# Filler matmuls of another size and number in the front of a fused linear-attention and gated-FFN kernel

## The chip, the core and the metric

The kernel runs on one core of a Trainium2 chip. The core has five engines with instruction streams of their own: TensorE (PE in the profile, with its weight loads as PEld), VectorE (DVE), ScalarE (ACT), GpSimd (POOL) and SyncE (SP). They meet through semaphores only. Sixteen DMA engines move data between the memory of the device and the core's on-chip memory; in this kernel SP and POOL issue the transfers. TensorE writes its results to PSUM, here eight banks of 128 partitions x 512 fp32 columns.

The metric is the time of one execution on the device in microseconds. A profiled execution also has a span, from the first to the last recorded instruction, which is a little shorter.

## The reference

Two parts, one after the other. The first is a gated linear attention over batch 4, 8 heads, 768 tokens and head dimension 48; the second is a feed-forward layer in which one projection is gated by the ReLU of another.

```python
f = 1.0 / (1.0 + np.exp(-f_logit))
for t in range(S):
    state = f[:, :, t, :, None] * state + np.einsum('bhd,bhe->bhde', k[:, :, t], v[:, :, t])
    y[:, :, t] = np.einsum('bhd,bhde->bhe', q[:, :, t], state)
...
x = y.transpose(0, 2, 1, 3).reshape(B * S, H * D)        # 3072 x 384
out = (np.maximum(x @ w_gate, 0.0) * (x @ w_val)) @ w_out  # 384 -> 1536 -> 384
```

## The kernel before

The sequence is cut into six chunks of 128 tokens. For each chunk and each pair of batches the attention is done in its chunked form. The logarithm of the gates is made on ScalarE (`bneg`) and summed over tokens by matmuls with triangular matrices (L594 for the first two chunks). Exponentials of the sums on ScalarE (L608) and products with k and q on VectorE and GpSimd (L610) give `hats`. TensorE transposes them (L642), VectorE copies them back (`qkT`, L650), and scores (L667), a mask (L683 on VectorE, L680 on GpSimd), the states (L692) and the output rows (L712, L717) follow. ScalarE writes these rows, transposed, as `xT` (L729). The feed-forward part of a chunk, for all four batches, reads `xT`: two projections on TensorE (L922), ReLU on ScalarE (L928), the product on VectorE (L932), the output projection on TensorE (L965, L945).

All matmul operands are bf16. Inputs are loaded by SP's queue (L487), in an order that is written out by hand; the weights come in three parts each through GpSimd's queue (L508), between GpSimd's computing steps: wg, wv, then wo. Some loads are written to wait for the landing of an earlier one.

The order of every engine's instructions is made by a small planner (class `Plan`): each operation has an estimated duration, a priority and tiles that it reads and writes; the planner simulates the engines and the DMA queues and gives each operation a start. From this it derives the order on each engine and the semaphore waits. An engine executes its list in this order, and a waiting instruction holds what stands behind it.

TensorE also gets *filler* matmuls. They multiply a tile of zeros with itself into the last PSUM bank, which the planner leaves alone until 15 us, and nobody reads their result. One of them (L1015) is an operation of the plan, at its start. The others are put in after planning: the loop over TensorE's order (L1027) looks at the planned gap ahead of each operation up to 15 us, and fills a share of it with matmuls of 512 columns. They are issued in front of that operation's semaphore wait (L1048), so TensorE works on them first and only then waits. In the order that results there are eighteen: two ahead of the matmul with `pick` (L434), seven ahead of the first sums (L594), six ahead of the first transposes (L642), one ahead of the scores (L667) and two ahead of the output rows (L712). The tile of zeros is cleared by VectorE's first instruction (`fill`, L415).

## Time and profile before

| | us |
|---|---|
| median of five runs | 192.71 |
| the five runs | 191.69, 192.32, 192.71, 194.14, 194.25 |
| the profiled execution, its time | 191.69 |
| its span | 190.0 |
| TensorE busy, share of the span | 182.5, 96% |
| first L594 matmul starts | 6.06 |
| first wv part waited for until | 17.63 |
| last wo part waited for until | 44.51 |

The page of the profile gives busy time per engine, groups of instructions by line, and the chain of waits that ended last. More detailed answers come from the trace: the chain in order of time, the timeline of one engine, and the work in a chosen stretch with the clock that TensorE was granted. In timeline rows the first number is the start in us from the beginning of the span, the second the time covered, then engine, line, operation, the tile written and the tiles read, the shape and the number of instructions. In brackets stands the idle time before and what ended it; "issue" there means that the profile shows nothing that was waited for.

### The profile page before, as it was taken

Reading aid. Unit: us, or ns where it says so; the run is one execution under the profiler, and the core shown is the slowest. Engines: PE = TensorE matmul, PEld = TensorE weight load, DVE = VectorE, ACT = ScalarE, POOL = GpSimd, SP = SyncE. Lnnn points to the kernel's source line nnn. Section 1 sums busy time; section 2 is a strip of 40 time slices with the busy share of each in tenths; the row PEclk is TensorE's granted clock in tenths of the full one; section 3 lists DMA queues with packets and bytes.
Section 4 is the critical chain, followed back from the end, with each engine's and each line's share of the span. In section 5 each row is a group of like instructions: output and inputs, shape, how many; then the busy total and the mean of one; then the engine's idle time right before and its main releaser. Section 6 shows DMA issues by size and latency. Waiting matters only on the chain.

```text
span 190.0 us, 5030 instructions
## 1 busy us (share of the span) xinstructions
PE 182.5 (96%) x2079; PEld 108.0 (57%) x2079; DVE 105.2 (55%) x189; ACT 109.6 (58%) x244; POOL 76.2 (40%) x109
## 2 busy tenths in 40 slices
PE   7887799999999999999999999999999999999994
PEld 2456684566685466768645564554555555554564
DVE  7799365995555856518695375625538233343300
ACT  3774459736598496575967739476533533334322
POOL 8496504771476638445393653615400000000000
PEclk9999999999999999999999999999999999999999
DMA  5999999999999999999999998999850310011113
GB/s 158 324 267 206 169 288 278 205 232 205 234 246 155 215 145 221 261 193 251 152 215 172 205 197 164 223 204 215 140 127 17 86 41 33 9 45 41 41 53 113
DMA packets 108854, 32.04 MB, mean 169 GB/s; under 512 B 101792, under 2 KB 108832, under 8 KB 108832
## 3 DMA queue, kind: packets, MB, share of 16 engines
q1 hardware_dynamic: 104848, 28.19, 73.5%
q0 software_dynamic: 3984, 3.54, 12.0%
q8 instruction: 16, 0.26, 0.5%
q14 instruction: 6, 0.05, 0.1%
HBM read 25.95 MB, written 4.72 MB: 161 GB/s over the span
## 4 chain that ended last, share of the span: by engine, by line
PE 82%; DMA 11%; POOL 3%; issue 1%; SPq 1%; ACT 0%; POOLq 0%
PE ps L922 48%; PE ps L965 23%; DMA wo<-in_moe_w_out_dram 5%; DMA wv<-in_moe_w_val_dram 4%; PE ps L852 3%; DMA q_in<-in_q_dram 2%; PE ps L817 2%; POOL hats L610 2%; PE ps L751 1%; PE ps L900 1%; POOL vpad L657 1%; PE ps L945 1%; PE ps L712 1%; SPq L487 1%; PE ps L754 0%
## 5 line engine op out<-in xcount | busy, mean ns | idle before, releaser
L932 DVE TENSOR_TENSOR gT<-relu,ps 128x512 bf16<-128x512 bf16 (+1 forms) x88 | 51.1, 588 | 61.0 <-PE ps L922 35.0
L928 ACT ACTIVATE relu<-ps 128x512 bf16<-128x512 f32 (+1 forms) x88 | 45.6, 522 | 28.2 <-PE ps L922 27.9
L922 PE MATMUL ps<-xT,wv 128*128 128x512 bf16 (+1 forms) x264 | 61.1, 340 | 0.4 <-DMA wv<-in_moe_w_val_dram 0.4
L922 PE MATMUL ps<-xT,wg 128*128 128x512 bf16 (+1 forms) x264 | 61.2, 340 | 0.0
L965 PE MATMUL ps<-wo,gT 128*128 128x384 bf16 x276 | 49.0, 326 | 0.2 <-DMA wo<-in_moe_w_out_dram 0.2
L965 PEld LDWEIGHTS ps<-wo,gT 128*128 128x128 bf16 x276 | 26.2, 98 | 18.2 <-DMA wo<-in_moe_w_out_dram 0.3
L922 PEld LDWEIGHTS ps<-xT,wv 128*128 128x128 bf16 x264 | 25.0, 98 | 19.6 <-DMA wv<-in_moe_w_val_dram 0.6
L922 PEld LDWEIGHTS ps<-xT,wg 128*128 128x128 bf16 x264 | 24.8, 98 | 19.5 <-issue 1.3
L975 ACT ACTIVATE osb<-ps 128x384 f32<-128x384 f32 x23 | 11.2, 495 | 26.2 <-PE ps L965 26.1
L827 DVE TENSOR_TENSOR ptm<-ps,tri 128x512 bf16<-128x512 f32 x32 | 20.5, 684 | 5.3 <-PE ps L817 5.2
L570 POOL TENSOR_TENSOR st<-ssum,dec 128x384 bf16<-128x384 f32 x16 | 13.1, 832 | 24.5 <-DVE ssum L568 24.4
L773 POOL TENSOR_TENSOR hats<-k_in,expo 128x384 bf16<-128x384 f32 x16 | 15.9, 1000 | 17.2 <-ACT expo L761 14.8
L777 POOL TENSOR_TENSOR hats<-q_in,expo 128x384 bf16<-128x384 f32 x16 | 15.7, 999 | 3.4 <-DMA q_in<-in_q_dram 3.3
L568 DVE TENSOR_TENSOR ssum<-ps,st 128x384 f32<-128x384 f32 x16 | 8.4, 553 | 3.7 <-PE ps L900 3.5
L683 DVE TENSOR_TENSOR ptm<-ps,mask 128x512 bf16<-128x512 f32 x14 | 8.7, 681 | 1.5 <-PE ps L667 1.4
L761 ACT ACTIVATE expo<-ps 128x384 f32<-128x384 f32 x16 | 7.9, 491 | 2.8 <-PE ps L754 2.7
L807 POOL CAST vpad<-v_in 128x384 bf16<-128x384 f32 x16 | 7.7, 507 | 1.8 <-DMA v_in<-in_v_dram 1.8
L763 ACT ACTIVATE expo<-ps 128x384 f32<-128x384 f32 x16 | 8.0, 500 | 0.0
L729 ACT ACTIVATE xT<-ps 128x384 bf16<-128x384 f32 x8 | 4.2, 599 | 5.4 <-PE ps L717 5.4
L742 ACT ACTIVATE f_in<-f_in 128x768 f32<-128x768 f32 x8 | 6.8, 844 | 0.9 <-DMA f_in<-in_f_logit_dram 0.9
L744 ACT ACTIVATE bneg<-f_in 128x768 bf16<-128x768 f32 x8 | 6.8, 846 | 0.1
L881 ACT ACTIVATE xT<-ps 128x384 bf16<-128x384 f32 x12 | 5.2, 486 | 2.5 <-PE ps L852 2.5
(85 smaller groups left out, 162.5 us busy)
## 6 DMA issues: line engine op xcount, KB each, us to landing
f_in<-in_f_logit_dram SPq DMA_DIRECT2D x12, 384.0 KB, 5.6
k_in<-in_k_dram SPq DMA_DIRECT2D x12, 384.0 KB, 5.4
q_in<-in_q_dram SPq DMA_DIRECT2D x12, 384.0 KB, 5.1
v_in<-in_v_dram SPq DMA_DIRECT2D x12, 384.0 KB, 5.4
out_dram<-osb SPq DMA_DIRECT2D x23, 192.0 KB, 2.4
wg<-in_moe_w_gate_dram POOLq DMA_DIRECT2D x3, 384.0 KB, 5.7
wv<-in_moe_w_val_dram POOLq DMA_DIRECT2D x3, 384.0 KB, 6.6
wo<-in_moe_w_out_dram POOLq DMA_DIRECT2D x3, 384.0 KB, 8.6
```

The lines of the kernel that those rows point to most:

```text
L568: add("DVE", lambda: ve.tensor_tensor(tmp[:, :], kv.ap[:, 0:HD], s_old[:, :], ALU.add), [kv, f"S{b}_{(c + 1) % 2}"], [key], prio=P + 8, ** ...
L570: add("POOL", lambda: gp.tensor_tensor(t4(s_new), t4(tmp), rate, ALU.mult), [key] + dk, [f"S{b}_{c % 2}"], prio=P + 8, **pool_t(HD))
L683: add("DVE", lambda i=i, j=j, mask=mask: ve.tensor_tensor(ptm[ms[i]][:, j, :, :], s[i][j].ap[:, :].rearrange("p (n t) -> p n t", n=NP), ma ...
L763: add("ACT", lambda: sc.activation(ex[:, 0, :], bc.ap[:, 0:HD], AF.Exp, scale=-1.0), [bc], [f"expq{ei // 2 * 2}_{ei % 2}"], prio=P + 1, ** ...
L773: add("POOL", lambda: gp.tensor_tensor(hk, kin[:, b % 2, :, :], ex[:, 1, :].rearrange("p (h d) -> p h d", h=H), ALU.mult), in_keys("k", c, ...
L777: add(e, lambda: engine[e].tensor_tensor(hq, qin[:, b % 2, :, :], ex[:, 0, :].rearrange("p (h d) -> p h d", h=H), ALU.mult), in_keys("q", ...
L827: add("DVE", lambda mi=mi, j=j, s=s: ve.tensor_tensor(ptm[mi][:, j, :, :], s.ap[:, :].rearrange("p (n t) -> p n t", n=NP), mask, ALU.mult) ...
L922: mm = te.matmul(bank.ap[:, 0:n], wt[:, kt, j * 128:(j + 1) * 128], xT[xi][:, kt, n0:n1], start=(kt == 0), stop=(kt == NK - 1))
L928: add("ACT", lambda: sc.activation(relu[ri][:, 0:n], gate.ap[:, 0:n], AF.Relu), [gate], [f"relu{ri}"], prio=P, **act_t(n))
L932: add("DVE", lambda: ve.tensor_tensor(gT[gi][:, j, n0:n1], relu[ri][:, 0:n], val.ap[:, 0:n], ALU.mult), [val, f"relu{ri}"], [f"gT{gi}_{j}_ ...
L965: mm = te.matmul(o[b].ap[:, 0:DM], gT[gi][:, j, b * C:(b + 1) * C], wo[:, j, :], start=(j == 0), stop=(j == NJ - 1))
L975: add("ACT", lambda b=b, oi=oi: sc.activation(osb[oi][:, :], o[b].ap[:, 0:DM], AF.Copy), [o[b]], [f"osb{oi}"], prio=P, **act_t(DM))
```

## The change

The fillers are no longer computed from the planned gaps by a formula. A list gives five groups, and each of the first five planned gaps over 0.4 us in TensorE's order takes one: nine fillers of 128 columns, eight of 512, five of 256, one of 512 and two of 512. With the filler that is part of the plan (now 128 columns wide) there are 26. They stand at the same five places as before. Columns beyond 128 are made by reading the same 128 columns of zeros again (a broadcast), so the tile of zeros has 128 columns instead of 512, and VectorE clears 64 words instead of 256 in each partition. The order of all real work is the same on all engines, but for two small clears of `dec` on VectorE that come before the products `upto` and `below` (L436) instead of after them.

```diff
-    zeros = sb("zeros", [128, 512], BF16)
+    zeros = sb("zeros", [128, 128], BF16)
...
-    fill("DVE", "zeros", zeros[:], 0.0, 256, -30)
+    fill("DVE", "zeros", zeros[:], 0.0, 64, -30)
...
-    WARM = 512
-    warm_until = 15.0
-    add("PE", lambda: te.matmul(banks[-1][:, 0:WARM], zeros[:, 0:128], zeros[:, 0:WARM]), ["zeros"], ["warm"], occ=0.2,
-        prio=-30)
+    add("PE", lambda: te.matmul(banks[-1][:, 0:128], zeros[:, :], zeros[:, :]), ["zeros"], ["warm"], occ=0.1, prio=-30)
...
-    def warm():
-        return te.matmul(spare[:, 0:WARM], zeros[:, 0:128], zeros[:, 0:WARM], start=True, stop=True, skip_group_check=True)
-
-    busy, at, begun = [], pl.free0["PE"], False
+    def warm(n):
+        return te.matmul(spare[:, 0:n * 128], zeros[:, :], zeros[:, :].unsqueeze(1).to_broadcast([128, n, 128]), start=True, stop=True,
+                         skip_group_check=True)
+
+    busy, at, wide = [], None, [(1, 9), (4, 8), (2, 5), (4, 1), (4, 2)]
     for op in order["PE"]:
-        gap, each = op.start - at, 0.44 if at < 4.0 else 0.23
-        if begun and op.start <= warm_until:
-            for _ in range(int((0.9 if gap > 1.5 else 0.6) * gap / each)):
-                busy.append((op, warm))
-        begun = True
+        gap = op.start - at if at is not None else 0.0
+        if wide and gap > 0.4:
+            n, many = wide.pop(0)
+            busy += [(op, lambda n=n: warm(n))] * many
         at = op.start + op.occ
```

## The prediction

> **What bounds the kernel now.** The profiled execution took 191.69 us: a span of 190.0 and 1.69 around it. The median of the five runs is 192.71, and they reach from 191.69 to 194.25, so the profile shows the best of them. I read the chain of waits first, in order of time, to learn where the front (the part before TensorE runs without a pause) touches the end.

> ```profile
> 7.54 1.00 POOL hats L610
> 8.55 0.90 POOL vpad L657 x2
> 9.45 0.88 POOL wg L508
> 10.32 7.30 DMA wv<-in_moe_w_val_dram
> ...
> 20.81 0.28 PE ps L717 x11
> 21.09 1.02 issue
> 22.11 0.22 PE ps L717
> ...
> 35.94 8.57 DMA wo<-in_moe_w_out_dram
> ```

> From 44.5 us on everything is TensorE, line after line, so the end is the moment at which that stretch starts plus about 143 us. Before it the chain runs through GpSimd (hats, vpad, then its weight transfers), through TensorE from 17.7 to 31.9 us, and through the last wo transfer. The fillers are not on it. They can move the end in two ways only: by the clock that they give the real matmuls, and by what stands behind them in TensorE's order. So I read the front's TensorE timeline next.

> ```profile
> 2.44 3.17 PE L1024 MATMUL ps<-zeros 128*128 128x512 bf16 x7
> ...
> 6.06 0.34 PE L594 MATMUL ps<-bneg,upto 128*128 128x384 bf16 x1 [0.46 <-ACT bneg L586]
> 6.23 0.33 PE L594 MATMUL ps<-bneg,below 128*128 128x384 bf16 x1
> 6.39 0.49 PE L594 MATMUL ps<-bneg,upto 128*128 128x384 bf16 x2
> 6.72 0.34 PE L619 MATMUL ps<-pick,bneg 128*128 128x2 bf16 x8
> 6.92 1.46 PE L1024 MATMUL ps<-zeros 128*128 128x512 bf16 x6
> 8.62 1.08 PE L642 MATMUL ps<-ident,hats 128*128 128x128 bf16 x16 [0.24 <-DVE hats L610]
> ```

> The seven fillers start (3.17 - 0.63)/6 = 0.42 us apart, 0.63 being the last one's length; the six later ones (1.46 - 0.38)/5 = 0.216. So the clock doubled between them, and the 384-column matmuls at 6.06 already start 0.165 apart, as everywhere later: in this execution the clock was up just in time for the first real work. The granted-clock column doesn't show the rise (it stands at 1.00 from the start), but it shows the fall after the last matmul:

> ```profile
> 15.81:19.22 3.41, 2.42 (x49) 1.00 1.24 205
> 186.48:189.89 3.41, 1.10 (x16) 1.00 0.33 115
> 189.89:189.96 0.07, 0.00 (x0) 0.51 0.00 0
> ```

> (Columns: stretch, its length, TensorE busy with count, granted clock, DMA share, GB/s.) A 3.41 us stretch with 1.10 us of work, 32%, ends with the clock halved; one with 2.42 us, 71%, keeps it.

> **The change part by part.**
> *Zeros tile.* 64 words instead of 256 to clear: the 0.27 us memset at 0.93 should take about as long as that of dec with 32 words, 0.09. The first filler starts near 1.07 instead of 1.26. VectorE's later steps move 0.18 us earlier, two dec memsets (0.13) go ahead of upto; upto waits for the pick matmul (2.22 + 0.28), and its reader on GpSimd is done long before 7.5 us. Worth nothing by itself.

> *First filler group, ten of 128 columns instead of two of 512.* At the slow clock 128 columns are 0.107 us (a quarter of 0.42). Ten fill 1.07 to 2.14; the pick matmul waits for GpSimd until 2.22 anyway. Cost nothing; the hole 2.08 to 2.22 nearly closes.

> *Second group, eight of 512 instead of seven.* Slow: 2.44 + 8 x 0.425 = 5.84 instead of 5.42. ScalarE's bneg releases the first real matmul at 6.05, so 0.2 us is left; the hole before it shrinks from 0.63 to 0.21. Cost nothing.

> *Third group, five of 256 instead of six of 512.* Fast: 5 x 0.108 = 0.54 instead of 1.29, so TensorE stands from about 7.5 to 8.6, where the transposes wait for VectorE's hats. Nothing gained in this execution, since the old group ended 0.24 before that wait did. The last three fillers stay.

> *What it is worth when the clock comes late.* [...] Estimate with the rise coming after 6.05: the four 384-column matmuls take 4 x 0.32 instead of 4 x 0.163, +0.63; the eight small ones +0.2; the six old fillers 6 x 0.425 = 2.55 instead of 1.29, +1.26. Transposes start at 6.06 + 1.28 + 0.4 + 2.55 = 10.3 instead of 8.6: 1.7 us late, and slower themselves. The new group costs 5 x 0.213 = 1.07: 8.8, behind the hats, which come at about 8.57 + 0.63 = 9.2. [...] Two of the five runs stand 2.5 us above the best, two 0.6 and 1.0: that is the size. I take for the new kernel most runs at the best one's time, some up to 0.6 above: 191.7 to 192.3.

> *Eight more matmuls shift the instruction stream.* TensorE's gap of 1.02 us "issue" at 21.09 lies inside one run of matmuls with no wait in it. Counting a load and a matmul each and the separate waits, it comes after instruction 706, and the only other gap of its kind (0.30 us, in L712 at 42.6) after 1218: 512 apart. The page's instruction queue moves 16 packets of 0.26 MB, 16 KB each. [...] So I take -0.1, with bounds -1.0 (the gap goes, none comes) and +0.5 (what follows the new gap is late too).

> Sum against the profiled execution: 191.69 + 0 (fillers, clock on time) - 0.1 (fetch) = 191.6; for the median of several runs plus 0.3 for those with a late clock: **191.9 us**, 0.4% under the median of before.

> **The rivals.**
> *Nothing moves, 192.7.* The spread then comes from transfers, not from the clock. For it: DMA is at 9 tenths through the whole front, and wv at 17.63 and wo at 44.51 are waited for. Against: these transfers start behind GpSimd's hats, which wait for ScalarE's expo and so for the very matmuls at 6.06.

> *Slower: the clock falls in the new hole.* Place: 7.45 to 10.86. Work there in the new order: 16 transposes x 0.056 = 0.90, state 0.37, one filler 0.21, scores 0.24: 1.72 of 3.41, 50%, where the old fillers made it 72%. It decides below some share between the 32% that lost the clock and the 71% that kept it. [...] Price: one window at half speed costs half of its 3.41 us, 1.7: 193.6; two, 195.3.

> *Clearly faster: the fetch gap goes and none comes in its place.* 191.69 - 1.02 = 190.7. [...]

> **How the numbers follow.** Forecast 0.50 (191.3 to 192.4), nothing 0.14 (192.4 to 193.2), slower 0.20 (193.3 to 195.3), clearly faster 0.16 (190.4 to 191.2). A measurement of this kernel tells about 1% from no change. The range 190.8 to 194.0 leaves out about half of each outer case. Faster by over 1% (under 190.8) 0.15, slower by over 1% (over 194.6) 0.13, within 0.72.

> **What would show it.** First filler near 1.07; eight fillers 0.42 apart to 5.8, or turning to 0.216 earlier; real matmuls at 6.06 0.165 apart; TensorE idle 7.5 to 8.6; transposes at 8.6 or, with a late clock, not beyond 9.3; five times within about 0.7 us of each other. [...] I am wrong if L642 or L667 after 10.9 run at double spacing, if the gap at 21 is gone, or if the five times spread as before.

## The result and the profile after

The changed kernel takes 192.87 us (median; 191.40 to 195.21), the kernel before, beside it on the same chip, 193.27 (191.57 to 196.34). The ratio is 0.9984 with a 95% interval of 0.9966 to 1.0002: 0.16% less, which can't be told from no change. The time lies inside the range of the prediction, which the width of that range allowed: the forecast was 191.9, the 0.4% did not come, and the times are spread over 3.8 us, not over 0.7.

The profiled execution of the changed kernel is one of its slow ones (194.68 us, 1.8 above its median), so its span of 193.0 us can't be set against the 190.0 of before; what it shows is where things stand in the front. TensorE's timeline after (start, time covered, engine, line, tiles, shape, count, idle time before):

```profile
1.06 0.29 PE L1013 MATMUL ps<-zeros 128*128 128x128 bf16 x1 [1.06 <-DVE zeros L415]
...
2.45 3.59 PE L1021 MATMUL ps<-zeros 128*128 128x512 bf16 x8
6.06 0.50 PE L594 MATMUL ps<-bneg,upto 128*128 128x384 bf16 x1
6.36 0.53 PE L594 MATMUL ps<-bneg,below 128*128 128x384 bf16 x1
...
7.56 0.71 PE L1021 MATMUL ps<-zeros 128*128 128x256 bf16 x5
8.95 1.08 PE L642 MATMUL ps<-ident,hats 128*128 128x128 bf16 x16 [0.68 <-DVE hats L610]
...
15.38 0.45 PE L642 MATMUL ps<-ident,hats 128*128 128x128 bf16 x5
18.40 0.50 PE L642 MATMUL ps<-ident,hats 128*128 128x128 bf16 x3 [2.56 <-issue]
...
19.68 1.07 PE L667 MATMUL ps<-qkT 48*64 48x128 bf16 x32
```

The eight fillers close the hole before L594. The L594 matmuls start 0.30 to 0.32 apart, twice as far as before: this is an execution in which the clock rose late, at 7.39 by the trace's clock records instead of 5.57. The transposes (L642) come 0.33 later than before (8.95 against 8.62). Then a gap without a releaser opens after five of the eight second transposes, 2.56 us long. The trace's clock records have the clock up from 7.39, at half from 17.63 and up again from 24.46, which is 10.24 and 6.83 us, three and two times 3.41. In stretches of that length (stretch, length, TensorE busy with count, loads, three other engines, granted clock, DMA share, GB/s):

```profile
7.39:10.80 3.41, 2.73 (x47) 1.92 (x45) 2.77 (x5) 3.01 (x8) 2.93 (x5) 1.00 1.17 325
10.80:14.22 3.42, 2.81 (x118) 1.82 (x122) 3.36 (x8) 2.67 (x8) 3.40 (x5) 1.00 1.18 231
14.22:17.63 3.41, 1.62 (x41) 1.16 (x35) 1.97 (x5) 1.06 (x2) 2.60 (x4) 1.00 1.22 197
17.63:21.05 3.42, 2.51 (x40) 1.72 (x41) 2.08 (x4) 0.98 (x2) 0.80 (x1) 0.50 1.00 167
21.05:24.46 3.41, 3.41 (x18) 2.43 (x16) 2.46 (x6) 0.77 (x2) 2.75 (x3) 0.50 0.98 138
```

The stretch that holds the gap is busy for 1.62 of 3.41 us, 47%, and after it the clock is at half for two stretches. The stretch in which the rival had it fall, 7.39 to 10.80, holds 2.73, 80%. The chain of waits after, to be read against that of before in the prediction:

```profile
7.87 1.00 POOL hats L610
8.87 0.90 POOL vpad L657 x2
9.77 0.88 POOL wg L508
...
15.84 2.56 issue
18.40 0.52 PE ps L642 x3
...
42.84 2.68 PE ps L965 x16
```

GpSimd starts the weights 0.32 later than before. The wait for wv is gone from the chain and the gap stands there, and in this execution TensorE's own work runs through to the end. What the gap and the halved clock cost here shows at the exponential (L608) that follows the sums of the next chunks (L594). GpSimd waits for it before it makes hats and issues the last wo load (first row before, second after):

```profile
32.49 2.27 POOL L610 TENSOR_TENSOR hats<-k_in,expo 128x384 bf16<-128x384 f32 x2 [0.98 <-ACT expo L608]
36.09 2.26 POOL L610 TENSOR_TENSOR hats<-k_in,expo 128x384 bf16<-128x384 f32 x2 [2.13 <-ACT expo L608]
```

The sums start at 34.99 instead of 31.39, so the last wo load is issued at 39.53 instead of 35.94 and lands at 46.87 instead of 44.51.

### The profile page after: what moved, and what is told of

Same layout as the page of the kernel before. It is cut to its first block, busy times and chain, and to the rows that moved or that the text cites. A ratio compares the mean times of both kernels' runs of the same rounds, so it can differ in the third digit from the quotient of the medians.

```text
span 193.0 us, 5045 instructions
## 1 busy us (share of the span) xinstructions
PE 185.4 (96%) x2087; PEld 110.6 (57%) x2087; DVE 105.3 (55%) x189; ACT 109.8 (57%) x244; POOL 76.2 (40%) x109
## 4 chain that ended last, share of the span: by engine, by line
PE 90%; POOL 3%; DMA 3%; issue 2%; SPq 1%; DVE 0%; ACT 0%; POOLq 0%
PE ps L922 50%; PE ps L965 23%; PE ps L852 3%; DMA q_in<-in_q_dram 3%; PE ps L817 2%; PE ps L642 2%; PE ps L712 2%; PE ps L751 1%; PE ps L900 1%; PE ps L667 1%; PE ps L945 1%; POOL wg L508 1%; PE ps L594 1%; PE ps L692 1%; POOL ptm L680 1%
## 5 line engine op out<-in xcount | busy, mean ns | idle before, releaser
L932 DVE TENSOR_TENSOR gT<-relu,ps 128x512 bf16<-128x512 bf16 (+1 forms) x88 | 51.3, 588 | 61.3 <-PE ps L922 35.9
L928 ACT ACTIVATE relu<-ps 128x512 bf16<-128x512 f32 (+1 forms) x88 | 45.6, 522 | 32.9 <-PE ps L922 32.5
L922 PE MATMUL ps<-xT,wg 128*128 128x512 bf16 (+1 forms) x264 | 62.5, 347 | 0.0
L922 PE MATMUL ps<-xT,wv 128*128 128x512 bf16 (+1 forms) x264 | 62.2, 345 | 0.0
L922 PEld LDWEIGHTS ps<-xT,wv 128*128 128x128 bf16 x264 | 25.5, 99 | 19.6 <-issue 0.2
L922 PEld LDWEIGHTS ps<-xT,wg 128*128 128x128 bf16 x264 | 25.4, 100 | 18.7
L642 PE MATMUL ps<-ident,hats 128*128 128x128 bf16 x64 | 4.8, 224 | 3.2 <-issue 2.6
L650 DVE COPY qkT<-ps 128x1024 bf16<-128x1024 bf16 x8 | 5.2, 677 | 3.6 <-PE ps L642 3.6
```

The source lines that it names most:

```text
L642: mm = te.transpose(t16[:, C * (2 * p + i):C * (2 * p + i + 1)], hats[:, his[i], x, 2 * p:2 * p + 2, :].rearrange("p h d -> p (h d)"), ide ...
L922: mm = te.matmul(bank.ap[:, 0:n], wt[:, kt, j * 128:(j + 1) * 128], xT[xi][:, kt, n0:n1], start=(kt == 0), stop=(kt == NK - 1))
L928: add("ACT", lambda: sc.activation(relu[ri][:, 0:n], gate.ap[:, 0:n], AF.Relu), [gate], [f"relu{ri}"], prio=P, **act_t(n))
L932: add("DVE", lambda: ve.tensor_tensor(gT[gi][:, j, n0:n1], relu[ri][:, 0:n], val.ap[:, 0:n], ALU.mult), [val, f"relu{ri}"], [f"gT{gi}_{j}_ ...
```

## The experiments

Each kernel was compared with the kernel before on the same chip, whose median there was 191.8 to 192.1 us, so 0.1% is 0.19 us. Beside the result it was 193.27: the chip, or the hour, moves the same kernel by more than the forecast did, so only comparisons on one chip count. A ratio with its interval is not the quotient of the two medians and differs from it by up to 0.3% (most for the ninety fillers, whose medians give 1.0026). Three theories were on trial: the clock sets the times of before (forecast; "theory 2" in the expectations); TensorE's gap without a releaser does (rival "clearly faster"; "theory 1", which supposes that a block of instructions comes late there; what holds TensorE there, no run shows); or transfers hide what TensorE gains (rival "nothing moves").

**The shift alone.** The kernel before, with eight matmuls of 16 columns after its second group of fillers:

```diff
+    second = list(fillers)[1]
+    fillers[second] += [lambda: te.matmul(spare[:, 0:16], zeros[:, 0:128], zeros[:, 0:16], start=True, stop=True,
+                                           skip_group_check=True)] * 8
```

> The kernel before with its eighteen fillers as they were, and eight more of 16 columns behind the second group, where TensorE would stand until 6.05 us anyway: the shift of the instruction stream alone. Theory 1 (blocks of instructions come late, and the number of instructions ahead sets where): TensorE's gap without a releaser leaves the last L717 matmul at 21 us and comes in the second L642 group near 15.3 to 15.6 us, at least 1 us long, as in the changed kernel; time as the changed kernel's, -0.5 to +0.3 us from before. Theory 2 (the clock that the fillers give sets the time): gap where it was in before, time as before.

Measured: 191.55 us, ratio 0.9990 (0.9971 to 1.0009). The gap left L717 and came to the second transposes, after five of eight, for 0.70 us. So the shift of sixteen instructions moves the stall, and is worth nothing that can be measured.

**The columns alone.** The changed kernel with its columns in eighteen fillers:

```diff
-    busy, at, wide = [], None, [(1, 9), (4, 8), (2, 5), (4, 1), (4, 2)]
+    busy, at, wide = [], None, [(4, 2), (4, 8), (3, 4), (4, 1), (4, 2)]
```

> The changed kernel with eighteen fillers instead of 26 but about the same columns in each group (1152 instead of 1280 in the first, the same 8 x 512 in the second, 4 x 384 instead of 5 x 256 in the third): the filling alone, the stream as long as before. Theory 1: the gap stands at the last L717 matmul, 1.0 to 1.5 us, none in L642 near 15.3; time as before within 0.4 us. Theory 2: all of what the change gives, -0.4 us from before, with a smaller spread of the times.

Measured: 191.80 us, 1.0010 (0.9983 to 1.0037), the gap (1.15 us) at the last L717 matmul as before. The denser filling without the shift gains nothing either.

**Next to no filling.** The changed kernel with all but the first filler 8 columns wide:

```diff
-        return te.matmul(spare[:, 0:n * 128], zeros[:, :], zeros[:, :].unsqueeze(1).to_broadcast([128, n, 128]), start=True, stop=True,
-                         skip_group_check=True)
+        return te.matmul(spare[:, 0:8], zeros[:, :], zeros[:, 0:8], start=True, stop=True, skip_group_check=True)
```

> The changed kernel with all 26 fillers in place but 8 columns wide (the planned one 128): the stream as in the changed kernel, next to no work on zeros. Theory 1 alone: the first sums run at the slow clock, +0.6 us on the changed kernel, gap in the second L642 group as there. Theory 2: the clock stays low through the front, +2 to +4 us, 195 to 197; real matmuls at double spacing until past 14 us.

Measured: 193.29 us, 1.0062 (1.0038 to 1.0087). The clock rises at 13.31 us, and a gap of 2.20 us stands in the second transposes. Against before this costs 1.2 us (0.7 to 1.7), between what the two theories gave. All fillers together are worth about this much.

**Ninety and sixty-eight fillers.** About the changed kernel's columns cut into narrower fillers, which need no broadcast, to push the gap elsewhere (144 and 100 instructions more than before). The second group, for one, is 32 of 128 columns in place of 8 of 512:

```diff
-        return te.matmul(spare[:, 0:n * 128], zeros[:, :], zeros[:, :].unsqueeze(1).to_broadcast([128, n, 128]), start=True, stop=True,
-                         skip_group_check=True)
...
+        return te.matmul(spare[:, 0:n], zeros[:, :], zeros[:, 0:n], start=True, stop=True, skip_group_check=True)
...
-    busy, at, wide = [], None, [(1, 9), (4, 8), (2, 5), (4, 1), (4, 2)]
+    busy, at, wide = [], None, [(128, 9), (128, 32), (64, 24), (64, 8), (64, 16)]     # ninety
+    busy, at, wide = [], None, [(128, 9), (128, 32), (128, 10), (64, 6), (64, 10)]    # sixty-eight
```

> [...] Theory 1: no gap without a releaser in TensorE's order between 13 and 24 us, at most one of up to 1 us near 49 us; -0.7 to -1.5 us from before, and a smaller spread. Theory 2: as the changed kernel, -0.4 us or nothing.

> The changed kernel's columns of zeros in 68 fillers of 128 and 64 columns: 100 instructions more than before. [...] Theory 1 (late blocks, and up to 44.5 us the wo transfer hides what TensorE loses): a gap without a releaser of about 1.4 us near 13.8 that costs little, and one of 0.5 to 1.1 us near 45.3 that nothing hides: +0.5 to +1.2 us on before. Theory 2 (only the filling counts): as the changed kernel, 0 to -0.4 us.

Measured: 192.37 us, 0.9996 (0.9967 to 1.0024), and 191.67 us, 0.9995 (0.9972 to 1.0018). With ninety no gap without a releaser is left between 13 and 24 us, and L594 at 31.39 starts at 30.28: the 1.1 us are there at 30 us, and gone at 45. With sixty-eight neither the gap of 1.4 us that I expected near 13.8 nor that near 45.3 came, only four of 0.2 to 0.3; these places were an estimate, and a count of instructions alone does not tell where TensorE stands. Where the gain of ninety went is in its chain of waits:

```profile
14.87 6.56 DMA wv<-in_moe_w_val_dram
...
22.48 8.29 DMA q_in<-in_q_dram
30.77 0.29 issue
31.06 0.43 POOL wo L508
...
32.62 2.50 POOL hats L610 x2
35.12 0.85 POOL vpad L657 x2
35.97 9.14 DMA wo<-in_moe_w_out_dram
45.11 0.05 issue
45.16 1.47 PE ps L965 x8
```

From 14.87 to 45.11 there is not one TensorE step in it. SP issues q_in when wv has landed; q_in lands 8.3 us later; GpSimd, which waits for it, then issues wo and makes hats and vpad, and the last wo comes after these. TensorE waits 1.24 us for it. In the chain of before, TensorE's own path (17.7 to 31.9, with the gap of 1.02 in it) met this one at the exponential of L608, which GpSimd's hats at 32.49 waited 0.98 for. GpSimd's wait for q_in in the two (before, ninety):

```profile
29.96 1.55 POOL L508 DMA_DIRECT2D wo<-in_moe_w_out_dram  x2 [8.45 <-DMA q_in<-in_q_dram]
31.06 1.55 POOL L508 DMA_DIRECT2D wo<-in_moe_w_out_dram  x2 [9.58 <-DMA q_in<-in_q_dram]
```

So the two chains differ by 0.98 us in before, and that much of the gap's 1.02 could have been gained there. With ninety fillers q_in, issued at the same time (22.48; 22.51 in before), landed 1.1 us later (30.77; 29.67), and the second chain became the end. In the eight profiles in which q_in was issued between 22.1 and 22.9 us it took 7.1 to 8.7 us to land; whether TensorE's lead lengthens it or chance does, no run shows.

**The last wo load moved up** behind the second on GpSimd's queue, in the kernel before, in the one with ninety fillers, and in the changed one:

```diff
+    line = order["POOL"]
+    wo1, wo2 = (next(op for op in line if op.writes == [nm]) for nm in ("wo1", "wo2"))
+    line.remove(wo2)
+    line.insert(line.index(wo1) + 1, wo2)
...
```

> The kernel before, fillers and TensorE's order untouched; on GpSimd's queue the third wo load stands right behind the second instead of behind two hats products and two vpad copies, so it is issued near 31.5 instead of 35.9 us. Theory 1 (two bounds side by side: the wo landing, and TensorE with its late block at 21 us, 0.2 us apart): wo is no longer waited for, and the end moves by what TensorE waited, 0 to -0.3 us. If the wo landing alone were the bound: -1 us or more.

> The ninety fillers (no late block at 21 us, but 1.24 us of waiting for wo) with the third wo load moved up in the same way. Theory 1: both bounds give way: -0.8 to -1.5 us from before, 190.4 to 191.1 where before is at 191.9; TensorE's wait for wo at 45 us falls under 0.4 us. If something else than these two set the start of the long stretch: as the ninety fillers alone, within 0.4 us of before.

> The changed kernel with the third wo load moved up in the same way. Theory 1: its late block sits in L642 near 15.6 us and delays TensorE's own order, so TensorE is the bound: 0 to -0.4 us from before. If the changed fillers do speed TensorE up and wo alone hid it: -0.6 us or more.

Measured: 192.13 us, 1.0007 (0.9989 to 1.0026); 192.15 us, 1.0008 (0.9990 to 1.0027); 191.95 us, 0.9999 (0.9978 to 1.0019). None gains. With ninety fillers TensorE is 0.84 us ahead of before at 44 us, 0.35 at 58, 0.11 at 85, and 0.51 behind from 112 on: its waits there are 0.6 in two for the transposed loads behind L817 (qkT), 0.2 for vpad, and 0.2 in one that shows no releaser. Of the 1.35 us lost since 44 us these are 1.0, and 0.6 of them are waits for transfers. The changed kernel with wo moved up shows both gaps at the places of the prediction, in L717 after three of twelve matmuls, eight earlier than before:

```profile
14.91 0.45 PE L642 MATMUL ps<-ident,hats 128*128 128x128 bf16 x5
16.28 0.34 PE L642 MATMUL ps<-ident,hats 128*128 128x128 bf16 x3 [0.92 <-issue]
...
21.04 0.24 PE L717 MATMUL ps<-qkT,st 128*32 128x128 bf16 x3
21.92 0.33 PE L717 MATMUL ps<-qkT,st 128*32 128x128 bf16 x9 [0.64 <-issue]
```

The first of these kernels (wo moved up in before) also shows, by luck, the old fillers with a late clock (the fillers' line is L1031 here).

```profile
5.95 0.50 PE L594 MATMUL ps<-bneg,upto 128*128 128x384 bf16 x1 [0.34 <-ACT bneg L586]
...
7.46 1.46 PE L1031 MATMUL ps<-zeros 128*128 128x512 bf16 x6
8.83 1.08 PE L642 MATMUL ps<-ident,hats 128*128 128x128 bf16 x16
```

The clock rises at 7.48. The L594 matmuls are slow, but the six fillers run fast, and the transposes start at 8.83, 0.21 later than with an early clock. The prediction had 10.3.

**The weights started later.** In the changed profile wv landed 1.66 us later (19.29 against 17.63) for an issue 0.32 later. To see whether a small delay grows, GpSimd clears an unread tile ahead of its first weight load, of 340 or 680 columns:

```diff
+    idle = sb("idle", [128, 340], BF16)
...
+            if nm == "wg" and s == 0:
...
+                    gp.memset(idle[:], 0.0)
             return gp.dma_start(dst, src)
```

> One GpSimd clear of a tile that nobody reads, in front of the first weight transfer; everything else is the kernel before. It moves the issue of all weight transfers by its own length, some 0.3 us (9.39 becomes about 9.7, the place where it stands in the changed kernel). If weight transfers set the end one for one: +0.3 us, the last wo landing 0.3 later. If the later start is amplified in the DMA queues (in the changed kernel wv came 1.7 us later for an issue 0.32 later): +1.5 to +2 us. If TensorE sets the end: 0, for wv's landing has no slack to hide in and then +0.3 as well, but wo's has; the landings tell.

> The same with a clear of twice the size, some 0.7 us. One for one: +0.7 us. Amplified: at least as much as the single clear, +1.5 to +2. A time that does not grow from the single to the double clear would say that the transfers' own rate and not their start sets the landings.

Measured: the first issue at 9.93 and 10.31 instead of 9.39; 192.13 us, 1.0021 (0.9998 to 1.0043), and 192.00 us, 1.0009 (0.9993 to 1.0025). The first wv part landed at 18.30 and 19.02, 0.67 and 1.39 later than in before, so the delay grows by up to a half in the transfers. It does not reach the end: a start 0.9 us later costs 0.5 us at most by its interval. TensorE's timeline tells where it is lost, in before (first two rows) and with the single clear (the lines there are L723 for L717 and L928 for L922):

```profile
22.11 0.22 PE L717 MATMUL ps<-qkT,st 128*32 128x128 bf16 x1 [1.02 <-issue]
22.25 0.50 PE L922 MATMUL ps<-xT,wg 128*128 128x256 bf16 x3
...
21.41 0.62 PE L723 MATMUL ps<-qkT,st 128*32 128x128 bf16 x12
21.96 0.50 PE L928 MATMUL ps<-xT,wg 128*128 128x256 bf16 x3
```

TensorE comes later, the gap of 1.02 us is gone, and behind its place TensorE is 0.3 us ahead of before (0.4 behind with the double clear). The gap at 706 takes up about 1 us of delay on the way to it, so the 0.3 us of a late clock on this path would not be seen.

**The late clock forced.** The changed kernel with its second group cut to 8 columns each:

```diff
+            slim = (n, many) == (4, 8)
-            busy += [(op, lambda n=n: warm(n))] * many
+            busy += [(op, lambda n=n, slim=slim: te.matmul(spare[:, 0:8], zeros[:, :], zeros[:, 0:8], start=True, stop=True,
+                                                           skip_group_check=True) if slim else warm(n))] * many
```

> The changed kernel with its second filler group (eight of 512 columns) cut to 8 columns each, so that TensorE is idle until 6.05 us and the clock rises late in every execution; the instruction count and all other fillers stay. By the prediction's step on the late clock the transposes come about 0.6 us late or more: +0.6 us. If what TensorE loses in the front only counts as far as it delays the weight issue: +0.3 us or less. With nearly no fillers at all the loss was 1.2 us, so this must lie between 0 and 1.2.

Measured: 192.48 us, 1.0040 (1.0016 to 1.0065), so +0.8 us (0.3 to 1.2). The clock rises at 12.35, and now the first transposes themselves are slow, and all that follows up to there:

```profile
8.87 1.89 PE L642 MATMUL ps<-ident,hats 128*128 128x128 bf16 x16
10.69 0.82 PE L692 MATMUL ps<-vpad,hats 64*128 64x96 bf16 x16
```

A rise after 12 us costs about what the prediction gave a late clock, 0.6. For a rise at 7.4 there are only single executions, since no kernel here holds it there; they show no cost.

**Less weight traffic.** The last wo load cut to a quarter, in the kernel before and in the one with ninety fillers:

```diff
-                          ap=[[DM, 128], [128 * DM, WJ], [1, DM]])
+                          ap=[[DM, 128], [128 * DM, 1 if s == 2 else WJ], [1, DM]])
```

> The kernel before with the last wo load cut to a quarter (96 of 384 KB; the output projection reads the one row block that is loaded in place of all four, so the output differs). Order and waits stay. If the front's end is the last wo landing alone, with no other bound near: the load lands 2 us or more earlier and the end comes with it, -1 to -2 us. If TensorE's own path is as late (moving this load up brought nothing): -0.1 to -0.3 us, TensorE no longer waits at 44.5 but starts there at nearly the same moment.

> The ninety short fillers, which bring TensorE about 1 us earlier to 30 us, with the same short wo load. If transfers take TensorE's gain back at 45 us and later: the traffic is now 288 KB (some 1.4 us at 200 GB/s) less, so the gain stays: -0.7 to -1.1 us against before. If the gain in the front is lost for another reason: within 0.3 us of before, as with ninety fillers and the load only moved up.

(In the second, too, the output projection reads the one block in place of four.) Measured: 191.53 us, 0.9973 (0.9952 to 0.9994), and 191.57 us, 0.9968 (0.9948 to 0.9989). 288 KB less in the front are worth about 0.5 us, more than any of the other sets of fillers gained over the old one. Neither expectation was met in full: the gain of the first (0.1 to 0.9 by its interval) can't be told from the -0.1 to -0.3 of TensorE's own path, and falls short of -1; the ninety fillers added next to nothing to it. In its profile their lead goes to the *second* wo load, which nobody shortened and which was issued behind a GpSimd wait of 9.38 us for q_in:

```profile
39.18 1.46 PE L965 MATMUL ps<-wo,gT 128*128 128x384 bf16 x8
41.70 1.47 PE L965 MATMUL ps<-wo,gT 128*128 128x384 bf16 x8 [1.05 <-DMA wo<-in_moe_w_out_dram]
```

## Why the prediction was right or wrong

**Zeros tile and first group: right.** The first filler starts at 1.06 (1.07 foretold); they were not tried alone, but with all columns changed and the shift left out nothing was gained (1.0010).

**Second group: right in worth, a little short in length.** Eight fillers cover 2.45 to 6.04, not to 5.84, because the last one's length is 0.63 and not 0.42. By the same slip the old hole was given as 0.63 us where the row said 0.46. L594 starts at 6.06 all the same.

**Third group: right.** TensorE stands for 0.68 us before the transposes and loses nothing by it.

**The late clock: the step that failed.** I let the clock stay low through the six old fillers and into the transposes, which gave 10.3 for them, and put the spread of the five times down to this; that was the 0.3 us and more of the forecast that did not come. No run shows the 0.3 us that the sum adds for it; what the runs showed in its place is a rise by 7.48 at no cost that is seen. Both halves fall. The rise did not come that late with the old fillers: in six profiles with the old widths (before, the shift alone, wo moved up in before, the two late starts, the short wo load in before) it comes at 5.57, 6.14, 7.48, 7.00, 6.68 and 5.94, in six with denser filling (after; eighteen; ninety alone, with wo moved up and with the short wo; sixty-eight) at 7.39, 6.10, 4.43, 4.78, 6.94 and 6.36; the changed one with wo moved up has no record of it. Whether it can come later with these fillers, no run shows. In the latest of the six old ones the six old fillers begin at 7.46, so the rise at 7.48 falls at their start, and not behind the 2.55 us that I gave them; the transposes then stood at 8.83. In the double late start the stretch ahead of the rise, 3.27 to 6.68, lies over the old hole, with 2.89 us busy, 85%. So in these profiles the old filling already did all that the new one does. Between 4.43 and 7.48 no cost of a later moment is seen: the span of before with wo moved up, at 7.48, is 189.9 us, that of before, at 5.57, 190.0 (two single executions), and what a later start costs on the way to the gap at 706 that gap takes up. The spread stayed (191.40 to 195.21), and no profile shows a first rise that would make it. What makes it remains open in the main. One part shows: the last wo landing differs by up to 2.7 us between the profiles (44.17 with eighteen fillers, 46.87 in after), and in the latest ones it is the issue that is late (39.53 us in after, 39.40 with next to no filling, 35.74 with eighteen), behind the exponential that a long gap and a fallen clock delay. But the 36 executions of the changed kernel whose clock did not fall reach from 191.40 to 195.21 too.

**The shift of the instruction stream ("fetch" in the sum): not contradicted in its worth, with no term for what the gap brought.** A new gap stands three matmuls before the end of the second transposes, and the old one moved eight matmuls forward or vanished. The new one was 2.56 us long in after, 2.20 with next to no filling, 1.19, 0.92 and 0.70 in others. Worth: no run shows the -0.1 of the sum; the shift alone measured -0.2 us (-0.6 to +0.2). The size matters: behind a gap of 2.56 us the clock is halved, for which the sum had no term. All three signs that the prediction named for being wrong came in the profile or the times: L667 at 19.68 runs at nearly double spacing (1.07 us for its 32 matmuls; 0.67 in before), the gap at 21 is gone, and the times spread as before.

**The rivals.** *Nothing moves* gave 192.7 and holds, at 192.87; of its reason, the transfers, the profiles show that these took what TensorE had gained in the front, not that they make the spread.

*Clearly faster* took the gap of 1.02 us, which stands on the chain of before at 21.09, to be worth its length. Ninety fillers remove it and gain 0.04% (between 0.24% lost and 0.33% gained): a second chain, through wv, q_in and wo, is within 1 us of it, and in the profile it took the gain. That it does so in every execution is argued, not shown.

*Slower by a fallen clock* named a fall that came, but not its place: the stretch from 7.39 to 10.80 kept the clock, with 2.73 us busy where 1.72 had been reckoned: the row gives 16 transposes 1.08 us, not 0.90, and 0.7 us of fillers were left out (in before such a stretch holds 3.02 us, 89%, not 72%). It fell behind the new gap instead, in three of the five profiles that have the gap in the second transposes (after, shift alone, next to no filling). There its price is seen: the sums at L594 start at 34.99, 33.66 and 34.86 us (30.3 to 32.7 in the other profiles), GpSimd waits 2.13, 1.28 and 1.89 us for the exponential behind them, and these executions are 1.8, 2.1 and 1.1 us above the medians of their kernels. The mean clock was below 0.995 in 16 of 116 executions of the five kernels with the gap there (8 of 44 of the changed one), and in 7 of 212 of the kernel before on the other chips. In the experiments 18 of 19 such executions lie 0.6 us or more above the median of the others of their kernel, the middle one 1.5; on the chip of the result, whose times spread more, the 8 have the same median as the others, 192.89. So this rival named a real cost, too rare to move the median. Whether the fall alone makes these executions long, or the gap as well, no run separates.

## What to carry to other kernels

An operation on the chain of waits is worth its length only up to the next chain, and the profile shows that one as well: follow the waits of the engine that feeds the chain's next step (here GpSimd's 0.98 us for L608) before you credit a gain, and allow for the other chain's own scatter (here q_in, 7.1 to 8.7 us). Before a spread of times is put down to a state, bound the earliest and latest moment of that state from what the rows show; here these were the rises at 5.57 to 7.48 us and the start of the fillers at 7.46. In this front filler matmuls are worth about 1.2 us: with them the clock was up by 7.5 us in the twelve profiles that show it, before the first transposes, and with next to none at 13.3; finer or denser ones were worth no more. And a gap can cost more than its own length: behind the one of 2.56 us the clock was at half for 6.83 us, and TensorE came 3.6 us later to the sums at L594 than before.
